# Retention and a four-expert layer on one core: where a batch's remainder is issued, and how a head pair's small matmuls are grouped

## The chip, the core and the metric

The kernel runs on one core of one Trainium2 chip. The metric is the device time in microseconds of one execution; less is better. Engines: TensorE (PE in the profile; its weight loads are PEld), VectorE (DVE), ScalarE (ACT), GpSimd (POOL) and SyncE (SP), which here only issues DMAs.

## The reference

Two stages, one feeding the other. Eight batches, eight heads, 576 positions, head size 64:

```python
scores = scale * np.matmul(q, k.transpose(0, 1, 3, 2))
gamma = 1.0 - 2.0 ** (-5.0 - np.arange(H))
Dmat = np.where(rel >= 0, gamma[:, None, None] ** rel[None, :, :], 0.0)
x = np.matmul(scores * Dmat[None], v)        # then heads side by side: [4608, 512]
p = domain_probs / (domain_probs.sum(-1, keepdims=True) + 1e-09)
for e in range(4):
    out += p[:, e:e + 1] * (np.maximum(x @ w1[e], 0.0) @ w2[e])
```

w1 is 512 x 1024 and w2 1024 x 512 for each of the four experts; rel is the distance of two positions.

## The kernel before

**Retention.** The decay gamma to the power of a distance is split into a factor for k (`gk`) and one for q (`gq`, applied to the output), so that within a chunk only a triangular mask is left. A batch's 576 positions are four chunks of 128 and a *remainder* of 64. Heads go in pairs, a head in each half of the 128 partitions. A `Pair` has these steps:

- `cast` (L227 on): k times gk to bf16 on VectorE, q and v to bf16 on ScalarE; `trans_dma`: SP issues two transposing DMAs into `qkT`.
- `scores` (L253): eight 64-row matmuls into a PSUM tile `s`, which VectorE masks into `sT` (L261).
- `kv` (L242): eight 64-column matmuls of running k^T v sums into a PSUM tile `kvp`, copied by ScalarE in two halves into the *states* `sbd` (L251).
- `values` (L265): into a PSUM tile `o`, eight matmuls of v with sT (L270) and then three of a state with q (L273), which add what earlier chunks contribute; VectorE multiplies by gq into `xt` (L280).

`Rem` does the same for the remainders of a batch's eight heads at once (scores L305, mask L306, values L311 and L313, `xt` L317). Batches 0 and 1 are done by `Unit`, four heads and two chunks at a time, with the same steps (L469 to L576).

**The experts.** Tokens go in nine tiles of 512. A tile takes 16 up groups, each eight 128x512 matmuls into one PSUM tile `ph` (L326; in tile 1 sixteen of 128x256, L344), evicted with Relu into `h` by ScalarE in tile 0 (L330) and by VectorE with the mixing weight `pB` in the others (L332, L347). Then the down products follow. Tile 0 has for each expert two groups of 16 matmuls, `po` (L359), between the up groups, evicted by VectorE into `acc` (L367, L369). The other tiles use a seven-product scheme on 256-token halves (`Down`): products 1, 4, 2, 5, 6, 3, 7, each 16 matmuls of 128x256 (L429), accumulate in one PSUM tile `pd` for a half; the sums of h that they need are made on VectorE (`sums`, L404 to L410). The corresponding sums of w2 are made once, on VectorE (`w_sum`, L378 to L384), while tile 0 ends and tile 1 begins.

**The order of the work.** Nothing is reordered by a planner (`tc.manual_schedule()`): each engine executes its instructions in the order in which the program issues them, and waits where a tile isn't ready. The program issues one group or product after another, and after the n-th it runs the functions put into *slot* n. A dictionary `slots` with hand-written numbers thus places every step of the retention between the groups of the experts. Tile 0 has 24 slots (per expert four up groups and two po groups), the other tiles 30 (16 up groups, then 14 products). While tile t is computed, the pairs of batch t + 1 and the remainder of batch t are done, since they give the columns of the tile after it.

In tile 0 the remainder of batch 0 is cast in slot 11, its scores in slot 15 and its values in slot 16; batch 1's units follow from slot 14 on, with SP's loads of the mixing weights `pB` for tile 1 in slot 17 (`load_p`).

**PSUM.** All these PSUM tiles come from one ring of four (`ring`, two banks each). A tile is handed on when its last reader has finished; `pd` holds one of the four for seven products.

**DMA.** SP's loads, transposes and stores go through one queue (q1), GpSimd's loads of weights and of x for batch 1 through another (q0).

Of the kernel before, what the change touches and what calls it, by code (L numbers as in the profile page):

```python
# [23 lines left out]
def kernel(  # L24
# [10 lines left out]
    nc = tc.nc  # L35
    B, H, S, D = q.shape
    N, E = moe_domain_probs.shape
# [3 lines left out]
    C = 128  # L41
    NC = 4
    SM = NC * C
    R = S - SM
    NP = H // 2
# [20 lines left out]
    def ring_tile(name, shape, dt=FP32):  # L66
        return ring.tile(shape, dt, tag="ring", name=name)
# [5 lines left out]
    def load_pair(t, b, p, eng=nc.sync):  # L73
        for n, src in srcs:
            for j in range(2):
                eng.dma_start(out=t[n][:, :, j, :],
                              in_=src[b, 2 * p + j, 0:SM, :].rearrange("(c p) d -> p c d", p=C))

    def load_rem(b, eng=nc.sync):
        for j in range(2):  # L80
            for n, src in (("k", k), ("v", v)):
                eng.dma_start(out=rawr[n][64 * j:64 * j + 64, :, j, :],  # L82
                                  in_=src[b, j:H:2, SM:S, :].rearrange("g t d -> t g d"))
        eng.dma_start(out=rawr["q"][0:R, :, :, :].rearrange("t g j d -> t (g j) d"),
                          in_=q[b, :, SM:S, :].rearrange("h t d -> t h d"))
# [5 lines left out]
    sbd = const.tile([128, NP, NC, 128], BF16, name="sbd")  # L91
# [117 lines left out]
    def load_p(t, e, eng):  # L209
        pB[t, e] = ppool.tile([128, NT], FP32, tag="pB", name="pB")  # L210
        eng.dma_start(out=pB[t, e], in_=pd[e:e + 1, t * NT:(t + 1) * NT].to_broadcast([128, NT]))  # L211
# [4 lines left out]
    def xt_of(t):  # L216
        if t not in xt:
            xt[t] = xpool.tile([128, NDC, NT], BF16, tag="xt", name="xt")
        return xt[t]


    class Pair:
# [39 lines left out]
                self.sT[:, :, :, :].rearrange("p j c t -> p (j c) t"), s[:, :, :, :].rearrange("p j c t -> p (j c) t"),  # L262
                tri[:, :].unsqueeze(1).to_broadcast([128, 2 * NC, C]), op=MULT)

        def values(self):  # L265
            b, p = self.b, self.p
            o = ring_tile("o", [128, SM])
            for c in range(NC):
                for j in range(2):
                    nc.tensor.matmul(o[64 * j:64 * j + 64, c * C:(c + 1) * C], lhsT=self.bf["v"][:, c, j, :],  # L270
                                     rhs=self.sT[:, j, c, :], start=(c == 0), stop=False, skip_group_check=True)
            for c in range(1, NC):
                nc.tensor.matmul(o[:, c * C:(c + 1) * C], lhsT=sbd[:, p, c - 1, :], rhs=self.qkT[:, 0, c, :],  # L273
                                 start=False, stop=(c == NC - 1), skip_group_check=True)
            n0 = b * S
            a = 0
            while a < SM:
                t = (n0 + a) // NT
                z = min(SM, (t + 1) * NT - n0)
                nc.vector.tensor_tensor(xt_of(t)[:, p, n0 + a - t * NT:n0 + z - t * NT], o[:, a:z],  # L280
                                        gq[:, p, a:z], op=MULT)
                a = z
# [37 lines left out]
    def up_group(h, t, e, i):  # L320
        ph = ring_tile("ph", [128, 2, NT])
        x = xt_of(t)
        for f in range(2):
            fc = 2 * i + f
            for dc in range(NDC):
                nc.tensor.matmul(ph[:, f, :], lhsT=w1_sb[e][:, dc, fc * 128:(fc + 1) * 128],  # L326
                                 rhs=x[:, dc, :], start=(dc == 0), stop=(dc == NDC - 1))
        fk = e * NFC + 2 * i
        if t == 0:
            nc.scalar.activation(h[:, fk:fk + 2, :], ph, Relu)  # L330
            return
        nc.vector.scalar_tensor_tensor(h[:, fk:fk + 2, :], ph, 0.0,  # L332
                                       pB[t, e][:, :].unsqueeze(1).to_broadcast([128, 2, NT]), op0=MAX, op1=MULT)
        if i == NFC // 2 - 1 and t + 1 < n_nt:
            load_p(t + 1, e, nc.gpsimd)

    def up_half(h, t, half, e, i):
        ph = ring_tile("ph", [128, 4, NT // 2])
        x = xt_of(t)
        c = slice(256 * half, 256 * half + 256)  # L340
        for f in range(4):
            fc = 4 * i + f
            for dc in range(NDC):
                nc.tensor.matmul(ph[:, f, :], lhsT=w1_sb[e][:, dc, fc * 128:(fc + 1) * 128],  # L344
                                 rhs=x[:, dc, c], start=(dc == 0), stop=(dc == NDC - 1))
        fk = e * NFC + 4 * i
        nc.vector.scalar_tensor_tensor(h[:, fk:fk + 4, c], ph, 0.0,  # L347
                                       pB[t, e][:, c].unsqueeze(1).to_broadcast([128, 4, NT // 2]), op0=MAX, op1=MULT)
        if half == 1 and i == 1:
            load_p(t + 1, e, nc.gpsimd)  # L350
# [280 lines left out]
    h = hp.tile([128, E * NFC, NT], BF16, name="h")  # L631


    def attention(slots, b, at):
        add = lambda i, f: slots.setdefault(i, []).append(f)
        for p, (c, s, o) in enumerate(at):
            x = Pair(b, p)
            add(c, lambda x=x: [x.cast(raw1, n) for n in "kqv"])
            add(c, x.trans_dma)
            if p + 1 < NP:  # L640
                add(c, lambda p=p: load_pair(raw1, b, p + 1))
            elif b + 1 < B:
                add(c, lambda: load_pair(raw1, b + 1, 0))
            add(s, x.scores)
            add(s, x.kv)
            add(o, x.values)

    def remainder(slots, b, at):
        add = lambda i, f: slots.setdefault(i, []).append(f)
        x = Rem(b)  # L650
        l, c, s, o = at
        if b > 0:
            add(l, lambda: load_rem(b))
        add(c, x.cast)
        add(c, x.trans_dma)
        add(s, x.scores)
        add(o, x.values)

    def run(slots, i):
        for f in slots.get(i, []):  # L660
            f()

    slots = {}
    add = lambda i, f: slots.setdefault(i, []).append(f)
    remainder(slots, 0, (-1, 11, 15, 16))

    def v_cast(u):
        vs[u].cast()
        vs[u].trans_dma()
        if u == 0:  # L670
            load_v(2, nc.gpsimd)
        elif u == 2:
            load_v(3, nc.gpsimd)
        elif u == 3:
            load_pair(raw1, 2, 0)

    def v_head(u):
        vs[u].scores()
        vs[u].kv()

    for u, (c, sc, o) in enumerate(((14, 18, 19), (17, 21, 22), (21, 24 + 0, 24 + 2), (24 + 0, 24 + 4, 24 + 6))):
        add(c, lambda u=u: v_cast(u))
        add(sc, lambda u=u: v_head(u))
        add(o, lambda u=u: vs[u].values())
    add(17, lambda: [load_p(1, e, nc.sync) for e in range(E)])
    for j in range(4):
        for wi, which in enumerate((3, 1, 2, 4)):
            add((17, 19, 22, 25)[j] + wi // 2, lambda which=which, j=j: w_sum(which, 4 * j, 4 * j + 4))
# [13 lines left out]
    for t in range(1, n_nt):  # L702
        slots = {i - 24: f for i, f in slots.items() if i >= 24} if t == 1 else {}
        if t < B:
            remainder(slots, t, (-1, 1, 6, 8) if t > 1 else (-1, 6, 10, 11))
        if t + 1 < B:
            attention(slots, t + 1, ((5, 10, 12), (10, 15, 17), (15, 19, 21), (19, 23, 25)) if t > 1 else
                      ((9, 14, 16), (14, 19, 21), (19, 23, 25), (23, 27, 28)))
        d = [Down(h, t, s) for s in range(2)]
        add = lambda i, f: slots.setdefault(i, []).append(f)  # L710
        add(12, lambda: d[0].sums(1, 0, HK))
        add(13, lambda: d[0].sums(2, 0, HK))
        add(14, lambda: d[0].sums(4, 0, HK))
        add(15, lambda: d[0].sums(1, HK, KH))
        add(16, lambda: d[0].sums(2, HK, KH))
        add(16, lambda: d[0].sums(4, HK, KH))
        add(17, lambda: d[0].sums(3, 0, HK))
        add(17, lambda: d[0].sums(3, HK, KH))
        for i, which in enumerate((1, 2, 4, 3)):
            add(19 + i, lambda which=which: d[1].sums(which, 0, HK))  # L720
            add(19 + i, lambda which=which: d[1].sums(which, HK, KH))
        run(slots, -1)
        n = 0
        for e in range(E):
            for i in range(4):
                if t == 1:
                    up_half(h, t, n // 8, n % 8 // 2, n % 2)
                else:
                    up_group(h, t, e, i)
                run(slots, n)  # L730
                n += 1
        for s in range(2):
            for m in (1, 4, 2, 5, 6, 3, 7):
                d[s].product(m)
                run(slots, n)
                n += 1
# [30 lines left out]
```

## Time and profile before

| | |
|---|---|
| median of 3 runs | 557.69 us (557.51 to 559.37) |
| the profiled execution | 559.56 us |
| its span, first to last instruction | 557.8 us |
| mean granted TensorE clock | 0.992 |
| TensorE busy | 535.8 us (96%) |
| VectorE busy | 375.6 us (67%) |
| ScalarE, GpSimd busy | 110.7 us, 55.0 us |
| DMA: moved, mean | 64.28 MB, 115 GB/s |
| tiles 2 to 6, each | 58.2 us |

"Busy" of TensorE counts from the start of a matmul to its modelled end, and matmuls overlap, so short distances between matmuls are read from their starts. In the profile a group of instructions is named by its line in the program, its engine, its operation, its output and inputs; "L259 PE MATMUL s<-qkT 64*128" is the matmul of line 259 with the array used as 64 rows by 128 columns. A wait is put down to what ended it.

### The profile page before, as it was taken

The numbers are of one execution on the slowest core, as the hardware profiler recorded it, in microseconds if no ns is written. First come the engines' busy times: TensorE is split into PE (matmuls) and PEld (weight loads), VectorE is DVE, ScalarE is ACT, GpSimd is POOL, SyncE is SP. The second block draws the span as 40 slices with busy tenths as digits, with TensorE's granted clock in tenths as the row PEclk, the third lists the DMA queues.
The fourth block names the chain that finished last, engine by engine and source line by source line (L and its number), as shares of the span: only waits on it lengthen the run. The fifth ranks groups of instructions, "written<-read, shape, count | busy, mean of one in ns | idle before, by whom it ended". The sixth has DMA issues, their size and how long they took to land.

```text
span 557.8 us, 10528 instructions
## 1 busy us (share of the span) xinstructions
PE 535.8 (96%) x4388; PEld 351.6 (63%) x4416; DVE 375.6 (67%) x550; ACT 110.7 (20%) x216; POOL 55.0 (10%) x95
## 2 busy tenths in 40 slices
PE   4999599999999999999999999999999999999996
PEld 3544245888854686468645874588447854884485
DVE  4622067988668874897389838984788567736871
ACT  5323323203211220212013201231113100000010
POOL 4613101010000000000000000000000000000000
PEclk9999899999999999999999999999999999999999
DMA  9999918456735752577155724753367131010010
GB/s 240 211 206 252 163 42 212 100 112 140 174 90 122 157 137 75 119 133 171 58 117 130 145 89 97 152 134 95 92 136 146 50 98 41 20 58 19 1 39 38
DMA packets 147454, 64.28 MB, mean 115 GB/s; under 512 B 127216, under 2 KB 137584, under 8 KB 147408
## 3 DMA queue, kind: packets, MB, share of 16 engines
q1 hardware_dynamic: 137760, 44.35, 35.2%
q0 software_dynamic: 9648, 19.27, 15.8%
q8 instruction: 34, 0.56, 0.4%
q14 instruction: 12, 0.10, 0.1%
HBM read 53.56 MB, written 9.51 MB: 113 GB/s over the span
## 4 chain that ended last, share of the span: by engine, by line
PE 91%; DMA 3%; DVE 2%; ACT 1%; issue 1%; SPq 1%; POOL 0%; POOLq 0%; DVEq 0%; ACTq 0%
PE ph L326 36%; PE pd L429 35%; PE po L359 5%; PE ph L344 5%; DMA qTr<-bfr_q 2%; PE kvp L246 2%; PE o L270 1%; PE s L259 1%; PE o L273 1%; PE kvp L525 1%; DMA rawr_q<-in_q_dram 1%; PE pt L483 1%; PE s L506 1%; ACT gq L157 1%; SPq L82 0%
## 5 line engine op out<-in xcount | busy, mean ns | idle before, releaser
L326 PE MATMUL ph<-xt,w 128*128 128x512 bf16 x1000 | 226.7, 381 | 1.4 <-DVE xt L570 0.2
L326 PEld LDWEIGHTS <-w 128*128 128x128 bf16 x1024 | 99.1, 98 | 115.1 <-issue 2.4
L332 DVE SCALAR_TENSOR_TENSOR h<-ph,pB 128x1024 bf16<-128x1024 f32 x112 | 136.2, 1221 | 31.6 <-PE ph L326 31.4
L429 PEld LDWEIGHTS <-h 128*128 128x128 bf16 x1024 | 98.8, 98 | 12.2
L429 PEld LDWEIGHTS <-s 128*128 128x128 bf16 x768 | 74.3, 98 | 8.9
L429 PE MATMUL pd<-wx,h 128*128 128x256 bf16 x512 | 61.2, 273 | 0.0
L429 PE MATMUL pd<-wx,s 128*128 128x256 bf16 x512 | 61.1, 273 | 0.0
L251 ACT ACTIVATE sbd<-kvp 64x256 bf16<-64x256 f32 x48 | 18.1, 378 | 112.1 <-PE kvp L246 111.8
L261 DVE TENSOR_TENSOR sT<-s,tri 128x1024 bf16<-128x1024 f32 x24 | 29.2, 1215 | 11.2 <-PE s L259 11.2
L211 POOL DMA_DIRECT2D pB<-pd x28 | 15.2, 542 | 206.3 <-DVE h L332 159.4
L455 POOL TENSOR_TENSOR ob<-v,p 128x256 f32<-128x256 f32 x16 | 11.6, 724 | 231.7 <-DVE v L452 139.4
L359 PE MATMUL po<-wx,h 128*128 128x512 bf16 x124 | 30.7, 401 | 0.2
L429 PE MATMUL pd<-t2w,s 128*128 128x256 bf16 x256 | 30.6, 273 | 0.0
L429 PE MATMUL pd<-t4w,h 128*128 128x256 bf16 x256 | 30.6, 273 | 0.0
L446 DVE TENSOR_TENSOR u<-pd,p 128x256 f32<-128x256 f32 x16 | 6.7, 422 | 35.4 <-issue 29.5
L429 PE MATMUL pd<-t3w,h 128*128 128x256 bf16 x256 | 30.6, 273 | 0.0
L344 PE MATMUL ph<-xt,w 128*128 128x256 bf16 x256 | 29.2, 273 | 0.3 <-DVE h L347 0.3
L280 DVE TENSOR_TENSOR xt<-o,gq 128x384 bf16<-128x384 f32 (+6 forms) x48 | 18.0, 415 | 16.4 <-PE o L273 16.4
L344 PEld LDWEIGHTS <-w 128*128 128x128 bf16 x256 | 24.6, 98 | 3.4 <-issue 0.3
L437 ACT ACTIVATE p<-pd 128x256 f32<-128x256 f32 x16 | 6.1, 384 | 96.1 <-PE pd L429 74.5
L330 ACT ACTIVATE h<-ph 128x1024 bf16<-128x1024 f32 x16 | 16.4, 1023 | 39.8 <-PE ph L326 38.0
L408 DVE TENSOR_TENSOR h<-h 128x1024 bf16<-128x1024 bf16 x32 | 23.4, 770 | 0.0
(130 smaller groups left out, 418.8 us busy)
## 6 DMA issues: line engine op xcount, KB each, us to landing
pB<-pd POOLq DMA_DIRECT2D x28, 256.0 KB, 3.7
raw_k<-in_k_dram SPq DMA_DIRECT2D x48, 128.0 KB, 2.9
raw_q<-in_q_dram SPq DMA_DIRECT2D x48, 128.0 KB, 3.4
raw_v<-in_v_dram SPq DMA_DIRECT2D x48, 128.0 KB, 3.3
w<-in_moe_w_dram POOLq DMA_DIRECT2D x4, 1024.0 KB, 13.5
wx<-in_moe_w_dram POOLq DMA_DIRECT2D x4, 1024.0 KB, 16.6
out_dram<-oa SPq DMA_DIRECT2D x16, 256.0 KB, 2.0
out_dram<-ob SPq DMA_DIRECT2D x16, 256.0 KB, 2.0
```

Source lines behind the costliest of these rows:

```text
L211: eng.dma_start(out=pB[t, e], in_=pd[e:e + 1, t * NT:(t + 1) * NT].to_broadcast([128, NT]))
L251: nc.scalar.activation(sbd[r, self.p, :, r], kvp[r, :, :], Copy)
L261: nc.vector.tensor_tensor(self.sT[:, :, :, :].rearrange("p j c t -> p (j c) t"), s[:, :, :, :].rearrange("p j c t -> p (j c) t"), tri[:, : ...
L280: nc.vector.tensor_tensor(xt_of(t)[:, p, n0 + a - t * NT:n0 + z - t * NT], o[:, a:z], gq[:, p, a:z], op=MULT)
L326: nc.tensor.matmul(ph[:, f, :], lhsT=w1_sb[e][:, dc, fc * 128:(fc + 1) * 128], rhs=x[:, dc, :], start=(dc == 0), stop=(dc == NDC - 1))
L330: nc.scalar.activation(h[:, fk:fk + 2, :], ph, Relu)
L332: nc.vector.scalar_tensor_tensor(h[:, fk:fk + 2, :], ph, 0.0, pB[t, e][:, :].unsqueeze(1).to_broadcast([128, 2, NT]), op0=MAX, op1=MULT)
L344: nc.tensor.matmul(ph[:, f, :], lhsT=w1_sb[e][:, dc, fc * 128:(fc + 1) * 128], rhs=x[:, dc, c], start=(dc == 0), stop=(dc == NDC - 1))
L359: nc.tensor.matmul(po[:, g, :], lhsT=h[:, e * NFC + fc, ns * 128:(ns + 1) * 128], rhs=wx[e // 2][:, (e % 2) * NFC + fc, :, :].rearrange("p ...
L408: nc.vector.tensor_tensor(h[:, l, self.b], h[:, l, self.a], h[:, l, self.b], op=SUB)
L429: mm = nc.tensor.matmul(dst, lhsT=src[:, kk, tok], rhs=rhs(c), start=(start and c == 0), stop=(c == KH - 1), skip_group_check=True)
L455: nc.gpsimd.tensor_tensor(self.ob[:, HF:Dm], self.v, self.p5, op=ADD)
```

## The change

Three edits.

1. The remainder of batch 0 is cast in slot 12 in place of 11, its scores are issued in slot 18 in place of 15, its values in slot 19 in place of 16. Unit 0 of batch 1 moves one slot back, from 18 and 19 to 19 and 20, so as to stay behind it. The four loads of pB for tile 1 move from slot 17 to slot 15.
2. `values` issues its three state matmuls first. It is given the next pair, and between the states and the eight matmuls with sT it issues that pair's scores and k^T v.
3. `attention` takes the slots of the casts and of these blocks apart: the first pair's scores and k^T v alone, then three joined blocks, then the last pair's values alone. In tiles 2 to 6 the casts stand in slots 5, 10, 15 and 20 (before: 5, 10, 15, 19) and the blocks in 10, 15, 20, 25 and 28 (before: scores in 10, 15, 19, 23, values in 12, 17, 21, 25). In tile 1 the casts stand in 8, 13, 18 and 22 and the blocks in 13, 18, 22, 26 and 28.

```diff
-        def values(self):
+        def values(self, following=None):
             b, p = self.b, self.p
             o = ring_tile("o", [128, SM])
+            for c in range(1, NC):
+                nc.tensor.matmul(o[:, c * C:(c + 1) * C], lhsT=sbd[:, p, c - 1, :], rhs=self.qkT[:, 0, c, :],
+                                 start=(c == 1), stop=False, skip_group_check=True)
+            if following is not None:
+                following.scores()
+                following.kv()
             for c in range(NC):
                 for j in range(2):
                     nc.tensor.matmul(o[64 * j:64 * j + 64, c * C:(c + 1) * C], lhsT=self.bf["v"][:, c, j, :],
-                                     rhs=self.sT[:, j, c, :], start=(c == 0), stop=False, skip_group_check=True)
-            for c in range(1, NC):
-                nc.tensor.matmul(o[:, c * C:(c + 1) * C], lhsT=sbd[:, p, c - 1, :], rhs=self.qkT[:, 0, c, :],
-                                 start=False, stop=(c == NC - 1), skip_group_check=True)
+                                     rhs=self.sT[:, j, c, :], start=False, stop=(c == NC - 1), skip_group_check=True)
...
-    def attention(slots, b, at):
+    def attention(slots, b, cast_at, head_at):
         add = lambda i, f: slots.setdefault(i, []).append(f)
-        for p, (c, s, o) in enumerate(at):
-            x = Pair(b, p)
+        xs = [Pair(b, p) for p in range(NP)]
+        add(head_at[0], xs[0].scores)
+        add(head_at[0], xs[0].kv)
+        for p in range(NP):
+            add(head_at[p + 1], lambda p=p: xs[p].values(xs[p + 1] if p + 1 < NP else None))
+        for p, c in enumerate(cast_at):
+            x = xs[p]
             add(c, lambda x=x: [x.cast(raw1, n) for n in "kqv"])
             add(c, x.trans_dma)
...
-            add(s, x.scores)
-            add(s, x.kv)
-            add(o, x.values)
...
-    remainder(slots, 0, (-1, 11, 15, 16))
+    remainder(slots, 0, (-1, 12, 18, 19))
...
-    for u, (c, sc, o) in enumerate(((14, 18, 19), (17, 21, 22), (21, 24 + 0, 24 + 2), (24 + 0, 24 + 4, 24 + 6))):
+    for u, (c, sc, o) in enumerate(((14, 19, 20), (17, 21, 22), (21, 24 + 0, 24 + 2), (24 + 0, 24 + 4, 24 + 6))):
...
-    add(17, lambda: [load_p(1, e, nc.sync) for e in range(E)])
+    add(15, lambda: [load_p(1, e, nc.sync) for e in range(E)])
...
-            attention(slots, t + 1, ((5, 10, 12), (10, 15, 17), (15, 19, 21), (19, 23, 25)) if t > 1 else
-                      ((9, 14, 16), (14, 19, 21), (19, 23, 25), (23, 27, 28)))
+            attention(slots, t + 1, *(((5, 10, 15, 20), (10, 15, 20, 25, 28)) if t > 1 else
+                                          ((8, 13, 18, 22), (13, 18, 22, 26, 28))))
```

## The prediction, made before the change was run

> **What bounds the kernel now.** I read the page's first part, then TensorE's waits, then the stretch of the longest wait, then one steady tile. The page says that TensorE is busy nearly throughout and that the chain of work is TensorE's.
>
> ```profile
> PE 535.8 (96%) x4388; PEld 351.6 (63%) x4416; DVE 375.6 (67%) x550; ACT 110.7 (20%) x216; POOL 55.0 (10%) x95
> ...
> PE 91%; DMA 3%; DVE 2%; ACT 1%; issue 1%; SPq 1%; POOL 0%; POOLq 0%; DVEq 0%; ACTq 0%
> ```
>
> So only three things can shorten it: TensorE waiting, its clock, and what it pays between matmuls. TensorE's list of waits has one large entry outside the start-up:
>
> ```profile
> PE sr L305 <- DMA qTr<-bfr_q: 7.5, 2, 6.8
> ...
> PE o L547 <- DVE sT L508: 0.3, 1, 0.3
> ```
>
> It is the remainder of batch 0 waiting for its transposed q. The stages around it (stretch, length, PE, PEld, DVE, ACT, POOL busy, granted clock, DMA share, GB/s):
>
> ```profile
> 59.40:66.40 7.00, 0.25 (x3) 0.08 (x3) 0.00 (x0) 2.51 (x5) 1.49 (x2) 0.85 1.30 155
> 66.40:72.20 5.80, 5.80 (x20) 2.28 (x21) 0.42 (x1) 0.00 (x0) 0.00 (x0) 0.60 0.27 74
> 72.20:76.00 3.80, 3.75 (x25) 1.88 (x25) 1.74 (x3) 0.00 (x0) 0.00 (x0) 1.00 0.02 4
> ```
>
> The reader is to see two losses: 6.75 us without matmuls, and after it a granted clock of 0.60, in which sixteen po matmuls take 5.70 us instead of 3.46 (427 ns from start to start, then 216). In the steady tile, TensorE's timeline around one pair (start, duration, count):
>
> ```profile
> 301.64 0.81 PE L326 MATMUL ph<-xt,w 128*128 128x512 bf16 x3
> 302.38 0.40 PE L259 MATMUL s<-qkT 64*128 64x128 bf16 x8
> 302.71 0.47 PE L246 MATMUL kvp<-bf_v,bf_k 128*64 128x256 bf16 x8
> ...
> 306.40 0.38 PE L429 MATMUL pd<-t4w,h 128*128 128x256 bf16 x2
> 306.71 0.41 PE L270 MATMUL o<-sT,bf_v 128*64 128x128 bf16 x8
> 307.06 0.34 PE L273 MATMUL o<-qkT,sbd 128*128 128x128 bf16 x3
> 307.23 0.27 PE L429 MATMUL pd<-wx,h 128*128 128x256 bf16 x1
> ```
>
> The third field after the line is the shape in which the array is used. The last ph starts at 302.07 and lasts 0.216, so s could start at 302.29; it starts at 302.38. The pd before the values could be followed at 306.62; o starts at 306.71. Within a shape two heads' matmuls follow at 53 ns; from s to kvp it is 146, from the values to the states 151. From the states back to pd, both 128*128, it is 56, the states' own time. A change of shape thus costs some 0.09 us, a return to the same shape nothing.
>
> [...] 0.09 us at each change, none where the shape stays. [...] 6.75 us idle, then 427 for 216 ns, for about 4.4 us. [...] the four transposes that SP issued from 54.76 to 59.47 land only from 64.6 to 68.2, beside GpSimd's weight and x loads.
>
> **The change, part by part.**
>
> *Remainder of batch 0 (cast 11 to 12, scores 15 to 18, values 16 to 19).* From the last ph of the third expert (59.44) to the next expert's first (75.92) there are 16.48 us. The work in it: 32 po at 0.216 = 6.91, the scores 0.18, the values 0.23, sum 7.32. Lost: 9.1 us, 6.75 of waiting, 2.24 of clock and 0.1 of restarting. After the change the scores stand behind two po groups and one ph group: 59.44 + 6.91 + 1.73 = 68.1. Do the transposes land by then? The k cast on VectorE has nothing else to wait for in slot 12 (TensorE's groups there are evicted by ScalarE), so it stays at 54.05. The q cast moves behind one Relu, from 46.74 to about 55.5, ends at 56.1, and SP reaches qTr at 56.16 anyway, since kTr occupies it until 56.06. So qTr lands at about 66.3, 1.8 us before its use. The next transposes (batch 1's first unit, landing 68.2) are used in slot 19, at 70.2. **Gain 9.1 us.** Cover: if these landings slip by over 1.8 us, the rest comes back as waiting.
>
> *What is late next.* The fourth expert now starts 9 us earlier against VectorE. From 66.6 it has the slot-17 acc (1.3), a k cast (0.6), two weight sums (1.3): 69.8, then sTr (0.4) at 70.2, while TensorE wants sTr at 70.0. I take **+0.3 us** (bounds 0 and 0.8, one more weight sum ahead). Unit 0's sT follows at about 73.0 and is wanted at 73.2; unit 1's transposes are issued at about 68 and 69.4 and wanted at 75.3.
>
> *The four pB loads (slot 17 to 15).* They need nothing that is late. SP issues them at 61 instead of 80.8, for 1.95 us, ahead of unit 1's transposes; SP is idle there. One MB took about 5 us in the trace (82 to 86). They follow the four transposes on SP's queue and share with two x loads until about 71, where DMA lay idle from 69 to 78. Unit 1's transposes then land near 74, 1.3 us early. I take **0**, bounds 0 and +1.
>
> *One block per pair.* Six batches with four pairs: before, 24 score blocks and 24 value blocks. Now the first scores and last values stand alone, and 18 blocks join the values of one pair with the scores of the next. States first continue the 128*128 shape; the values follow k^T v in the same 128*64 shape. Removed per joined block: one entry into the values (0.09) and one return from k^T v (125 ns where 53 is the pace, 0.07): 0.17 us, at most 0.19. **Gain 18 x 0.17 = 3.1 us** (2.9 to 3.4), all on TensorE, so on the path. A block takes 0.82 + 0.61 - 0.17 = 1.26 us. No matmul is added; VectorE's and ScalarE's evictions are the same, later by some slots.
>
> *The wait that it adds.* The ring has four PSUM tiles. In slot 15 of tiles 2 to 6 the block takes three (o, s, kvp), so the first product, in slot 16, needs that of the last ph group. Its eviction cannot end before 0.20 (a group that ended at 292.21 has its eviction start at 292.41) + 1.22 = 1.42 us after the group; with the sums ahead of it VectorE's timeline has
>
> ```profile
> 301.96 0.68 DVE L410 TENSOR_TENSOR s<-h,s 128x1024 bf16<-128x1024 bf16 x1
> 302.56 1.22 DVE L332 SCALAR_TENSOR_TENSOR h<-ph,pB 128x1024 bf16<-128x1024 f32 x1
> ```
>
> an end at 303.78, 1.49 after the group's 302.29. The block covers 1.26. With 0.06 for the signal TensorE waits **0.3 us in each of five tiles: +1.5**. Behind it stands everything, TensorE being in order. Bounds: 0, and 0.75 where the tile handed on is kvp's (two ScalarE copies of 0.38 after k^T v). Other blocks lie in the product stage, where the next product keeps its tile; tile 1's first block too.
>
> *Casts and buffers.* A pair's cast is now issued after the block that reads its buffers; the v cast and the transposes wait for that block, but ScalarE and VectorE are held to TensorE there by their evictions. Cast to scores stays five slots (four for tile 1's last two), over 8.7 us. The last values move from slot 25 to 28; slot 29 (1.75 us) and three ph matmuls cover their 0.76 us eviction. 0.
>
> *Sum.* -9.1 - 3.1 + 1.5 + 0.3 = -10.4. The profiled execution took 559.56 (span 557.8), giving 549.2; the median of the runs is 557.69, 1.87 below it, giving **547.3 us**. Bounds: 557.69 - 9.1 - 3.4 = 545.2; 557.69 - 9.1 - 2.9 + 3.8 + 0.8 + 1.0 = 551.3.
>
> **The rivals.**
>
> *The wait moves to unit 1.* The pB loads stand ahead of its transposes. If those then take the 10.0 us that qTr took, they land at 79.4, 4 us late, enough for the clock to drop again (another 2.2): 547.3 + 6.2 = 553.5. For it: such a landing did occur. Against: then a 1 MB weight load and several x loads were in flight, now only two x loads. 0.10.
>
> *The joined block saves nothing,* [...]: 547.3 + 3.1 = 550.4. Against: states to pd shows 56 ns. 0.10.
>
> *Slower: every block waits for VectorE.* Place: the first matmul after a block, or the block's own o, if the tile it needs is that of s or of an older o. VectorE ends sT 2.6 us and xt 3.3 us after the group, 1.3 to 2.0 beyond the block: 18 x 1.3 = 23.4, so 557.7 - 12.2 + 23.4 + 0.3 = 569.2. It decides from 12.2 / 18 = 0.68 us per block. Against: at 13 of 18 blocks the next matmul opens no tile, and before the change TensorE shows no wait for a steady tile's PSUM. 0.03.
>
> **How the numbers follow.** Forecast 0.77, rivals 0.10, 0.10, 0.03. The range 545.2 to 551.3 takes in the forecast's bounds and the second rival; about 0.15 is left out. Half a per cent (554.9 to 560.5) is what a measurement can tell from no change: faster 0.95, same 0.02, slower 0.03.
>
> **What would show it.** No TensorE wait at L305 near 68 us and a granted clock of 1.00 from 30 to 90 us; the fourth expert's first ph near 66.4; in a joined block kvp to o at about 53 ns and ph to o without a gap; a wait of 0.3 us before the first pd in tiles 2 to 6, on the eviction of ph. Wrong if unit 1's scores wait for qkT, or if the wait at pd is over 0.7 us.

## The result, and the profile after

The changed kernel takes a median of **551.84 us** (four runs: 550.04, 550.35, 553.33, 553.64) where the kernel before took 557.6 (four runs, 557.31 to 559.37): a ratio of 0.989, 95% interval 0.9843 to 0.9937. So it is faster by more than half a per cent, as forecast, but the median lies 0.5 us above the range (545.2 to 551.3) and 4.5 above the 547.3 predicted. The profiled execution is the one of 550.04 us, span 548.2, granted clock 1.0; it stands against 559.56 before. In the changed kernel the lines behind `values` are numbered 3 higher; within it the states' matmuls are L269 and those with sT L276.

The first part of the page, and its chain of work:

```profile
PE 530.7 (97%) x4388; PEld 354.1 (65%) x4416; DVE 376.4 (69%) x550; ACT 110.1 (20%) x216; POOL 55.4 (10%) x95
...
PE 74%; DMA 8%; DVE 7%; SPq 5%; ACT 3%; issue 2%; POOL 0%; POOLq 0%; another core or an unknown queue 0%; ACTq 0%; DVEq 0%
```

TensorE is still busy nearly throughout, but its share of the chain fell from 91% to 74%: the chain now leaves it at several small waits and goes back through VectorE, the loads and SP. TensorE's waits from the first expert on (in all, times, longest):

```profile
PE pd L432 <- DVE h L335: 1.7, 5, 0.8
PE sr L308 <- DMA qTr<-bfr_q: 0.5, 1, 0.5
...
PE pd L432 <- ACT p L440: 0.3, 1, 0.3
PE s L509 <- DMA qkT<-bf_q: 0.3, 1, 0.3
PE pd L432 <- ACT oa L443: 0.3, 1, 0.3
```

The 6.75 us are gone. What is left of `sr` (0.5, before 0.7) is the remainder of a later batch. In its place stand five waits of the first product of a tile for VectorE (four of 0.22 us and one of 0.83), and single ones of 0.3 us. The three stretches shown of before, now:

```profile
59.40:66.40 7.00, 6.96 (x33) 3.00 (x32) 1.41 (x2) 2.53 (x5) 1.49 (x2) 1.00 1.21 222
66.40:72.20 5.80, 5.28 (x62) 2.91 (x62) 5.36 (x10) 2.05 (x2) 0.00 (x0) 1.00 1.17 182
72.20:76.00 3.80, 3.75 (x33) 1.68 (x34) 3.68 (x6) 1.78 (x3) 0.00 (x0) 1.00 0.59 168
```

In the first, TensorE is busy 6.96 of 7.00 us where it was 0.25; in the second the clock is 1.00 where it was 0.60. The DMA engines, nearly idle in the third row before, are now loaded until past 72 (third row: share 0.59, before 0.02). A joined block in tile 3, from TensorE's timeline:

```profile
233.58 0.81 PE L329 MATMUL ph<-xt,w 128*128 128x512 bf16 x3
234.23 0.33 PE L269 MATMUL o<-qkT,sbd 128*128 128x128 bf16 x3
234.49 0.40 PE L259 MATMUL s<-qkT 64*128 64x128 bf16 x8
234.82 0.47 PE L246 MATMUL kvp<-bf_v,bf_k 128*64 128x256 bf16 x8
235.12 0.39 PE L276 MATMUL o<-sT,bf_v 128*64 128x128 bf16 x8
235.73 0.27 PE L432 MATMUL pd<-wx,h 128*128 128x256 bf16 x1 [0.22 <-DVE h L335]
```

The last ph starts at 234.01 (the group's first, 233.58, and two more at 0.216) and would end at 234.23, where the states begin: no gap on entry. From the first k^T v matmul to the first of the values it is 0.30 us; before, to the product that followed, it was 0.40 (302.71 to 303.11). From the start of the last k^T v matmul to the values it is 25 ns now, and was 125. The bracket at the end is the wait that the change adds.

From the first ph of one tile to the next (us):

| | tiles 0 and 1 | tiles 2 to 5, each | tile 6 | tile 7 | the rest |
|---|---|---|---|---|---|
| before | 133.28 | 58.23 | 59.14 | 52.43 | 50.34 to the start of the last product |
| after | 124.66 | 57.83 (one 58.88) | 58.97 | 52.21 | 50.34 |

That is -8.62, -0.55, -0.17 and -0.22: -9.56 of the span's 9.6. Tile 0 alone went from 69.97 to 61.57. (Tile 6 took 59.14 before, not the 58.2 that the table ahead of the change gives for tiles 2 to 6.)

### The profile page after: what moved, and what is told of

It is laid out like the page before. It is cut to its first block, busy times and chain, and to the rows that moved or that the text cites. A ratio compares the mean times of both kernels' runs of the same rounds, so it can differ in the third digit from the quotient of the medians.

```text
span 548.2 us, 10530 instructions
## 1 busy us (share of the span) xinstructions
PE 530.7 (97%) x4388; PEld 354.1 (65%) x4416; DVE 376.4 (69%) x550; ACT 110.1 (20%) x216; POOL 55.4 (10%) x95
## 4 chain that ended last, share of the span: by engine, by line
PE 74%; DMA 8%; DVE 7%; SPq 5%; ACT 3%; issue 2%; POOL 0%; POOLq 0%; another core or an unknown queue 0%; ACTq 0%; DVEq 0%
PE pd L432 32%; PE ph L329 29%; PE po L362 4%; DVE h L335 4%; PE ph L347 3%; DMA raw_v<-in_v_dram 3%; SPq L76 2%; DMA qkT<-bf_q 2%; SPq L239 2%; PE kvp L528 1%; DMA raw_k<-in_k_dram 1%; PE kvp L246 1%; PE o L276 1%; PE s L259 1%; PE s L509 1%
## 5 line engine op out<-in xcount | busy, mean ns | idle before, releaser
L432 PE MATMUL pd<-wx,s 128*128 128x256 bf16 x512 | 61.2, 273 | 0.1
L261 DVE TENSOR_TENSOR sT<-s,tri 128x1024 bf16<-128x1024 f32 x24 | 29.3, 1220 | 16.6 <-PE s L259 16.6
L362 PE MATMUL po<-wx,h 128*128 128x512 bf16 x125 | 28.5, 379 | 0.2
L372 DVE SCALAR_TENSOR_TENSOR acc<-po,pm,acc 128x512 f32<-128x512 f32 x12 | 8.5, 746 | 24.0 <-PE po L362 24.0
```

Source lines behind the costliest of these rows:

```text
L261: nc.vector.tensor_tensor(self.sT[:, :, :, :].rearrange("p j c t -> p (j c) t"), s[:, :, :, :].rearrange("p j c t -> p (j c) t"), tri[:, : ...
L362: nc.tensor.matmul(po[:, g, :], lhsT=h[:, e * NFC + fc, ns * 128:(ns + 1) * 128], rhs=wx[e // 2][:, (e % 2) * NFC + fc, :, :].rearrange("p ...
L432: mm = nc.tensor.matmul(dst, lhsT=src[:, kk, tok], rhs=rhs(c), start=(start and c == 0), stop=(c == KH - 1), skip_group_check=True)
```

## The theory, and what could be wrong with it

My theory after this result: the mechanism is the one forecast, and the pair of profiles (-9.5 against -10.4) bears it out; the median is higher because in part of the executions a wait returns in tile 0, at batch 1's unit 0 or with its clock. Rivals: that the pB loads, moved ahead, cause it (the first rival of the prediction, at another place); that the joined blocks or the PSUM ring cost more than one profile shows; that the first four runs were an accident. The experiments ran on several chips; each is compared with the kernel before on its own chip. They go by labels: a1 to a4, b1 to b4, c1 to c4, d1 and d2, in the order in which they stand here. A "wait at L509" is that of TensorE at unit 0's scores.

## Experiments: each part alone

**The changed kernel again** (a1, no edit).

> The changed kernel once more, unaltered. Its four runs stood at 550.0 and 550.4 us with a granted clock of 1.00 and at 553.6 and 553.3 us with 0.992 and 0.993. Theory C (a half-clock stretch that falls into some executions): the runs come again in two groups about 3.3 us apart, and the group goes with the clock. Theory D (late loads or stores of SP, no clock): the times spread without a gap and the clock doesn't order them.

Measured: 549.68 us (six runs, 549.28 to 554.3) against 559.29, ratio 0.9859 (0.982 to 0.9898). In four of the six the mean granted clock is 0.998 to 1.0 and the time 549.3 to 549.7; the other two are 551.93 (clock 0.997) and 554.3 (0.992). So the spread is real, and in these six the clock orders the times. The two groups 3.3 us apart don't come again as such, and over more runs the clock alone doesn't order them: c1 below has 553.68 us at 0.997 and 552.23 at 0.995, so waits count beside it.

**The remainder alone** (a2): the kernel before with the three edits of tile 0.

```diff
-    remainder(slots, 0, (-1, 11, 15, 16))
+    remainder(slots, 0, (-1, 12, 18, 19))
-    for u, (c, sc, o) in enumerate(((14, 18, 19), (17, 21, 22), ...
+    for u, (c, sc, o) in enumerate(((14, 19, 20), (17, 21, 22), ...
-    add(17, lambda: [load_p(1, e, nc.sync) for e in range(E)])
+    add(15, lambda: [load_p(1, e, nc.sync) for e in range(E)])
```

> Kernel before with the remainder of batch 0, unit 0 and the pB loads moved, pairs untouched. My steps: the 6.75 us wait and the 2.24 us of half clock go, up to 0.3 comes back behind sTr: tile 0 (to the first ph of tile 1) from 69.97 to about 61.2 us, the whole some 8.5 us shorter, 548.5 to 549.5. If the half-clock stretch comes from the joined blocks, this kernel has one group of times only; if it comes from the start of the kernel or from the first tile, it has two.

Measured: 552.25 us (551.28 to 557.21), ratio 0.9896 (0.9859 to 0.9932): -7.0 us. Its tile 0 takes 61.56 us, as in the changed kernel (61.57); the tiles after it take what they took before. The forecast of 548.5 to 549.5 was missed: the 8.5 us were again taken from a median. Between the two profiled executions (559.56 and 551.28) they are 8.3. One of the six runs stands at 557.21 with a clock of 0.993, so slow executions come without joined blocks, too.

**The joined blocks alone** (a3): the changed kernel with those three lines put back.

> Kernel before with the joined blocks alone, remainder at its old slots. My steps: 18 x 0.17 us less, about 0.3 us of waiting in each of tiles 2 to 6: tiles of 57.8 in place of 58.2 us, the whole 1 to 2 us shorter (555.5 to 556.5). If a shape change costs nothing that a joined block can save: 1.5 us longer than before. If late SP loads bite (the 0.8 us wait of tile 4 in the changed kernel), one or more tiles are 58.9.

Measured: 557.12 us (555.05 to 560.59), ratio 0.9971 (0.9954 to 0.9989): -2.2 us. The two parts add up: -7.0 - 2.2 = -9.2, together -9.6 (a1), within what the intervals allow. Tiles 3, 5 and 6 take 57.83 us each, as forecast (57.8). The wait at the remainder, which this version keeps, can be read in its profiled execution, which took 555.05; first from TensorE's waits, then from two stretches:

```profile
PE sr L308 <- DMA qTr<-bfr_q: 4.8, 2, 4.4
```

```profile
59.50:65.00 5.50, 1.07 (x10) 0.38 (x8) 0.27 (x1) 2.81 (x5) 1.49 (x2) 1.00 1.19 193
65.00:68.50 3.50, 3.50 (x10) 1.27 (x9) 0.15 (x1) 0.00 (x0) 0.00 (x0) 0.51 0.44 108
```

The same wait is 4.4 us here, not 6.75, and is followed by 3.5 us at a clock of 0.51, where the trace of before has 6.83 us at 0.50 (from 64.25); tile 0 takes 67.39 us, not 69.97. Tile 0 is the same code in both. The size of the loss that the change removes differs from one execution to the next.

**The pB loads back in slot 17** (a4), in the changed kernel.

```diff
-    add(15, lambda: [load_p(1, e, nc.sync) for e in range(E)])
+    add(17, lambda: [load_p(1, e, nc.sync) for e in range(E)])
```

> Changed kernel with the four pB loads back in slot 17. My step: they cost nothing at 15, so within 0.3 us of the changed kernel. Rival (the loads stand ahead of unit 1's transposes): unit 0's scores wait 0.3 us less for qkT, and up to 1 us is gained; or the loads now stand behind unit 1's transposes and nothing moves.

Measured: 551.29 us (548.1 to 554.41), ratio 0.9861 (0.9822 to 0.99), where the changed kernel had 0.9859 on the same chip (the median is 1.6 us higher, the mean of the six runs 0.3). The spread stays. Unit 0's transposes land 11.3 to 13.0 us after their issue with the loads late, 12.0 to 13.8 with them early (a1). Moving the pB loads is worth nothing that can be measured, and they are not what delays unit 0.

## Experiments: the small waits

**The first half's x loads issued four slots later** (b1), in all tiles with attention. In the changed kernel the last pair's cast stands in slot 20, where the first stores also fall due. SP's timeline in tile 4 of the changed kernel:

```profile
306.15 1.19 SPq L239 DMA_TRANSPOSE qkT<-bf_k  x1
307.44 1.21 SPq L239 DMA_TRANSPOSE qkT<-bf_q  x1
308.71 1.12 SPq L76 DMA_DIRECT2D raw_k<-in_k_dram  x2
309.88 1.91 SPq L76 DMA_DIRECT2D raw_q<-in_q_dram  x2
311.88 1.00 SPq L76 DMA_DIRECT2D raw_v<-in_v_dram  x2
312.99 0.45 SPq L452 DMA_DIRECT2D out_dram<-oa  x1
```

and what waits for that store on ScalarE:

```profile
315.84 0.38 ACT L443 ACTIVATE oa<-pd 128x256 f32<-128x256 f32 x1 [5.83 <-DMA out_dram<-oa]
```

The store of oa is issued after two transposes and six loads, 6.8 us after the first of them; ScalarE waits 5.83 us for oa's buffer, and its next eviction of pd (0.3 us on TensorE here, up to 1.1 in a4) comes late.

```diff
-                add(c, lambda: load_pair(raw1, b + 1, 0))
+                add(c + 4, lambda: load_pair(raw1, b + 1, 0))
```

> Changed kernel with the six loads of the next batch's first pair issued four slots later, behind the stores of the first half of a tile. Theory S (the stores stand on SP's queue behind the last pair's transposes and these loads, which the change moved one slot closer to them; ScalarE's copy oa waits for the store, and the product after it for the copy): the waits of TensorE on oa and p, 0.3 to 1.6 us in the four traces with joined blocks, go. If the store itself is slow to land, they stay.

Measured: 552.8 us, one run. SP now issues the store right behind the transposes:

```profile
310.60 1.21 SPq L239 DMA_TRANSPOSE qkT<-bf_q  x1
311.90 0.53 SPq L452 DMA_DIRECT2D out_dram<-oa  x1
313.60 2.00 SPq L76 DMA_DIRECT2D raw_k<-in_k_dram  x2
```

and in tiles 2 to 6 the waits on oa and p are gone; one of 0.3 us on p is left. The time says nothing on that: this execution had a wait of 2.6 us at L509 with half clock after it (eight ph matmuls take 3.3 us from 74.24 on, the eight from 78.03 on 1.8). All nine traces with joined blocks and without this edit have a wait on oa or p; of the four with it (b1, b4, c4, d2) only b1 has one, the 0.3 us.

**The second block one slot later** (b2), so that it doesn't stand just before the first product.

```diff
-            attention(slots, t + 1, *(((5, 10, 15, 20), (10, 15, 20, 25, 28)) if t > 1 else
+            attention(slots, t + 1, *(((5, 10, 16, 20), (10, 16, 20, 25, 28)) if t > 1 else
```

> Changed kernel with the first joined block of tiles 2 to 6, and the cast of the third pair, in slot 16 in place of 15, so that the first product has its PSUM tile before the block takes three. My step (the block's three tiles leave the product only that of the last ph): the five waits of 0.22 us for VectorE's h, 1.1 us in all and 1.7 us where a load came late, go, tiles of 57.6 in place of 57.8 us. If they belong to VectorE's backlog and not to the ring, they reappear at the next product.

Measured: 548.61 us, one run. The five waits of the first product for h are gone; TensorE's list from 140 us on is

```profile
PE sr L308 <- DMA qTr<-bfr_q: 0.7, 1, 0.7
PE pd L432 <- ACT oa L443: 0.4, 1, 0.4
PE s L259 <- DMA qkT<-bf_q: 0.3, 1, 0.3
```

and a steady tile takes 57.56 us, not 57.83. The wait is thus worth 0.27 us per tile, and the three joined blocks alone (58.23 - 57.56) / 3 = 0.22 us each.

**Remainder and units one slot later still** (b3) in tile 0.

```diff
-    remainder(slots, 0, (-1, 12, 18, 19))
+    remainder(slots, 0, (-1, 12, 19, 20))
-    for u, (c, sc, o) in enumerate(((14, 19, 20), (17, 21, 22), ...
+    for u, (c, sc, o) in enumerate(((14, 20, 21), (17, 22, 23), ...
```

> Changed kernel with the scores and values of the remainder and of units 0 and 1 one more slot back. Theory L (the slow executions are those in which the transposes of tile 0 land late, so that TensorE waits and the clock drops): wait for qkT of 0.3 to 0.8 us gone, no run above 552 us, median near 549. Theory C (a half-clock stretch with no wait of its own behind it): one run in three still near 553.5 us with a clock of 0.992.

Measured: 550.21 us (four runs, 549.18 to 550.47), ratio 0.9822 (0.9775 to 0.987). The runs lie close together, but the profile contradicts the expectation: in the execution of 550.44 us the wait at L509 is not gone but 2.0 us, since unit 0's transposes landed 14.6 us after issue, 1 to 3 us later than in the changed kernel's first two traces; and unit 1's values, now in the last slot of tile 0, make the next tile's first group wait 1.1 us for xt. More distance alone didn't cure it.

**All four edits at once** (b4: the three above, and the pB loads in slot 17).

> All of it: the later loads, the block in slot 16, the remainder one more slot back, and the pB loads in slot 17. Sum of the waits that they should take out of the changed kernel's profile: 0.6 (oa, p) + 1.7 (h) + 0.3 (qkT) + 0.2 (sTr), 2 to 3 us: 547 us, where the clock stays at 1.00. If the waits only move, 549 to 550.

Measured: 548.97 us (547.58 to 552.26), ratio 0.9811 (0.9773 to 0.9849). TensorE's waits from 60 to 90 us:

```profile
PE s L509 <- DMA qkT<-bf_q: 2.7, 1, 2.7
PE ph L347 <- DVE xt L573: 1.1, 1, 1.1
```

The steady tiles are clean; tile 0 isn't.

## Experiments: why unit 0's transposes land late

**The changed kernel a third time** (c1), on another chip.

> The changed kernel a third time, to stand beside the next kernel on the same chip. Theory L (unit 0's transposed q lands late in some executions; TensorE waits, and where the wait is long the clock drops): some runs near 549.5 us, some 2 to 5 us above. A trace of a slow one shows the wait at unit 0's scores.

Measured: 554.17 us (550.38 to 555.12), ratio 0.9889 (0.9853 to 0.9925). Its profiled execution, of 552.23 us, shows the event. TensorE's timeline, then two stretches:

```profile
68.56 1.89 PE L329 MATMUL ph<-xt,w 128*128 128x512 bf16 x8
...
72.24 0.42 PE L509 MATMUL s<-qkT 64*64 64x128 bf16 x16 [1.56 <-DMA qkT<-bf_q]
```

```profile
66.00:73.80 7.80, 5.92 (x65) 3.11 (x64) 6.35 (x10) 2.53 (x4) 0.00 (x0) 1.00 1.17 207
73.80:77.30 3.50, 3.50 (x26) 1.36 (x25) 1.60 (x4) 1.30 (x2) 0.00 (x0) 0.51 0.38 80
```

A wait of 1.56 us, then 3.5 us at a clock of 0.51, which lose half of that, 1.7 us. Against the execution a1 showed (a wait of 0.79 there and no drop) that makes 0.77 + 1.7 = 2.5; its tile 0 took 64.19 us against 61.49, and the whole 552.23 against 549.72. No execution of the changed kernel above 552.23 us was traced; that the seven runs from 553.3 to 555.1 lose their time in the same way, with a longer wait or a second stretch, is not shown.

**Unit 2's x loads left out**, in the changed kernel (c2) and in the kernel before (c3). Unit 2 then works on unit 0's data.

```diff
-        if u == 0:
-            load_v(2, nc.gpsimd)
-        elif u == 2:
+        if u == 2:
             load_v(3, nc.gpsimd)
```

> Changed kernel that leaves out the three x loads for unit 2 (768 KB, issued by GpSimd from 55 to 61 us; unit 2 then works on unit 0's data), which share the DMA engines with the remainder's and unit 0's transposes. Theory L: those transposes land earlier, unit 0's scores never wait over 0.3 us, and the runs stay within 1.5 us of their fastest, near 549. If the slow executions have another cause (the start of the kernel, stores, the clock by itself): the same spread as the changed kernel, up to 554.

> Kernel before without the same three loads. Theory L: its long wait is the landing of the remainder's transposes, so it shrinks from 6.8 us (to 3 or 4, since the weight load of expert 3 is still in flight), and with it the clock's stretch: 554 to 556.5 us, with less spread than the 556.5 to 562.7 of the kernel before. If the loads don't matter: the same 559.

Measured: the changed kernel without them 548.48 us (five runs, 547.69 to 549.45), ratio 0.9802 (0.977 to 0.9834); the kernel before without them 557.04 (556.09 to 560.08), ratio 0.9956 (0.994 to 0.9972). In the first there is no wait at unit 0's scores, its transposes land 5.5 to 7.0 us after their issue, and tile 0 takes 61.03 us. Its slowest run is faster than the fastest of c1, on the same chip, where unit 0's transposes took 12.7 to 13.0 us. In the second the wait at the remainder is still

```profile
PE sr L305 <- DMA qTr<-bfr_q: 5.1, 2, 4.5
```

So these loads delay unit 0's transposes in the changed kernel. Leaving them out is worth 2.6 us to the kernel before. Its wait was 6.75 us in one trace with these loads and 4.4 in another (a3), so the 4.5 here doesn't show that they lengthen it; but it stands without them, too: for that the remainder had to be moved.

**The same loads on SP's queue** (d1), behind unit 0's transposes, in the changed kernel. Nothing is left out; the bytes are the same.

```diff
         if u == 0:
-            load_v(2, nc.gpsimd)
+            load_v(2, nc.sync)
```

> Changed kernel with unit 2's three loads issued by SP, behind unit 0's transposes, in place of GpSimd. If the loads delay the transposes [...]: unit 0's transposed q lands 6 to 8 us after its issue as without the loads (12 to 17 us in the changed kernel), no wait at unit 0's scores, all runs between 547.5 and 550 us. If it is the bytes: still late landings in some executions, runs up to 554 us.

Measured: 549.79 us (six runs, 549.1 to 550.79), ratio 0.9832 (0.9804 to 0.9861). The spread shrank from 5.0 us (a1) and 4.7 (c1) to 1.7, and all six have a clock of 0.998 to 1.0. Three of the six lie a little above the 547.5 to 550 that was expected. The changed kernel wasn't run on this chip, and the intervals of the ratios overlap; what differs is the spread. There is no wait at L509. Unit 0's transposes, which took 12.7 to 13.0 us from issue to landing in c1, take here

```profile
DMA to landing us min/median/max: 4.8/5.6/6.4
```

The stretches from 66 to 74 us show the same; in c1

```profile
66.00:70.00 4.00, 3.68 (x21) 1.61 (x20) 3.52 (x6) 1.02 (x1) 0.00 (x0) 1.00 1.17 106
70.00:74.00 4.00, 2.44 (x47) 1.64 (x45) 3.02 (x6) 1.71 (x3) 0.00 (x0) 0.98 1.18 310
```

and with the loads on SP's queue

```profile
66.00:70.00 4.00, 4.00 (x24) 1.88 (x22) 2.80 (x5) 1.02 (x1) 0.00 (x0) 1.00 0.96 315
70.00:74.00 4.00, 3.81 (x53) 1.95 (x51) 3.96 (x7) 1.78 (x3) 0.00 (x0) 1.00 0.34 70
```

In c1 the DMA engines are as full from 66 to 70 us (share 1.17) but move 106 GB/s: unit 0's transposes, issued at 57.1 and 59.2, are still running and land at about 70 and 72. Their packets are small: in the trace of before, from 62 to 66 us, SP's queue, on which only transposes were issued from 54.76 to 78.19, moved 0.28 MB in 1150 packets, some 240 bytes each. In d1 they are through by 66.3, and the loads of x and pB run at 315 GB/s four microseconds earlier. In c1 both queues moved packets from 50 to 80 us, GpSimd's for 53.7% of the engines' time and SP's for 46.1%; how an engine divides its time between them was not shown. What the two traces show is the landing: at the median 5.6 us after issue with the loads behind the transposes on one queue, 12.8 with them on the other. They don't separate the order from the kind of queue, as GpSimd's was replaced by SP's, nor from the time: the first of the loads is issued at 61.2 us here and at 55.3 in c1.

**The best put together**: the x loads four slots later, the second block one later, the remainder in slots 19 and 20 with units (14, 20, 21) and (17, 21, 22), pB in slot 17; then the same with unit 2's loads on SP's queue (c4 and d2).

> All of b4 but unit 1 at its slots of the changed kernel, so that the tile-1 wait of 1.1 us for its xt, which b4's trace showed, goes: 1 us below b4 in the same circumstances, 547 to 548 us; by theory L still some runs 3 us above.

> The kernel of c4 with the same edit. Without the late landings its runs should all stand where its best three stood, 546.5 to 548 us; if the loads now come late for unit 2, a wait of 1 to 2 us appears at the start of tile 1 and it is 548 to 550.

Measured: the first 548.69 us (546.48 to 551.09), ratio 0.9806 (0.977 to 0.9842), with a wait in its profiled execution (550.77 us) of

```profile
75.18 0.42 PE L509 MATMUL s<-qkT 64*64 64x128 bf16 x16 [3.85 <-DMA qkT<-bf_q]
```

and the second **547.78 us** (546.79 to 548.14), ratio 0.9793 (0.9763 to 0.9824), the lowest median of all versions, with a spread of 1.35 us where the first has 4.6. The ratios don't tell the two apart. In its profile (546.79 us, span 545.1) TensorE waits from the first expert on for no more than

```profile
PE s L259 <- DMA qkT<-bf_q: 0.3, 1, 0.3
PE ph L347 <- DVE h L350: 0.3, 1, 0.3
PE sr L308 <- DVE bf_k L230: 0.2, 1, 0.2
```

## Why the prediction was right and wrong

547.3 us were predicted and 551.84 measured. Of the 4.5 us between them, 1.9 come from the last step of the sum (from 549.2 down to 547.3), 0.9 from its terms (549.2 against the 550.04 of the profiled execution) and 1.8 from the distance of the median from that execution, where the cover failed (the parts are rounded). Each in turn below.

**Remainder of batch 0: right.** -9.1 and +0.3 were forecast for tile 0; it went from 69.97 to 61.57, -8.4. No wait at the remainder, clock 1.00, the fourth expert's first ph at 66.57 where 66.4 was forecast. The +0.3 for sTr came as 0.2, and unit 0's scores waited 0.3 beside it.

**Joined block: right in kind, too small.** 0.17 us each was forecast, 0.22 measured (57.56 against 58.23 for three). The entry has no gap, as forecast; the return from k^T v to a matmul of the same shape gained 0.10 us where I took 0.07 (25 ns remain, not 53). So 18 blocks would gain 4.0, not 3.1; that holds for the 15 in tiles 2 to 6, while tile 1 with its three got only 0.22 shorter, not 0.67, which stays open. The rival that they save nothing falls: from the last k^T v matmul (128*64) the traces show 125 ns to the start of one of another shape (128*128) and 25 to one of the same.

**PSUM ring: right.** Five waits of the first product on the eviction of ph, 0.22 us in four tiles and worth 0.27 a tile by b2 (forecast 0.3); in one tile 0.83, where VectorE had waited 0.81 us for a raw_k that was loaded late. That one is over the 0.7 named as a sign of being wrong; b2 shows that the ring is its place, too. In tile 3 the eviction ends at 235.68 and TensorE starts at 235.73: 0.05 us for the signal, where 0.06 was taken. The rival that every block waits falls.

**"Casts and buffers ... 0": wrong.** A cast brings its DMAs. One slot later, the last pair's put two transposes and six loads on SP ahead of the first stores; ScalarE then waits for oa's buffer and TensorE for ScalarE, 0.6 us in this profile, up to 1.8 in others (a4). b1 removed all but 0.3. I had cost the cast on VectorE and ScalarE and not on SP.

**pB loads: right, 0** (a4). The first rival put the new wait at unit 1 behind these loads. Nothing waited there. Of its kind, though, an event came: a wait at unit 0's scores, and half clock behind it (1.56 us, then 3.5 us at 0.51 in c1).

**The cover: wrong, and with it the median moved by 1.8.** The prediction took from one trace that unit 0's transposes land at 68.2, 2.0 us before their use, and that the cover of the remainder is 1.8. That landing is not a constant. Issue to landing was 8.7 to 9.2 us in the trace of before, 11.5 to 13.2 in the first of the changed kernel, 15.4 in b4, up to 16.6 in c4: waits at L509 from none (a4) to 3.9 us, with or without 1.7 of clock behind them. Of the 16 runs of the changed kernel seven are between 549.3 and 550.4 and nine between 551.9 and 555.1. c2 against c1 shows that unit 2's x loads, issued from 55 to 61 us on the other queue, are a cause: without them none of five runs was above 549.5, where c1 had 550.4 to 555.1. In the twelve runs of d1 and d2 the same bytes did no such harm behind the transposes on SP's queue. The loads alone don't decide: with them, a2 and a3 had landings of 6.6 to 7.7. The text did name the condition ("if these landings slip by over 1.8 us, the rest comes back as waiting"), but gave it no chance and no place in the range.

**The last step of the sum: wrong.** From the profiled execution, -10.4 gave 549.2; measured in the pair, 550.04. I then took off another 1.87 because the median of the three runs lay that much below. But the loss that was removed is what those executions differ by. Of 76 runs of the kernel before over four sessions, those with a mean clock of 0.997 (11) average 557.2 us, those at 0.992 (24) 559.3 and those at 0.989 (16) 561.4. A stretch like that of a3, 3.5 us at a clock of 0.51, takes 0.003 off the mean clock of such a run (3.5 x 0.49 / 558), so these are, by estimate from that and from the mean clocks, runs with one, two and three times this loss (the last two also with some at the very end: a clock of 0.64 from 555.0 to 557.8 in the trace of before, another 0.002). The profiled execution had 0.992 and twice the loss, 6.83 us at 0.50; two of the three runs shown were some 2 us shorter, and so had less to win. The wait was 6.75 in one execution and 4.4 in another (a3). A loss that varies can't be taken whole from a median that holds only part of it: 549.2 was the estimate for an undisturbed execution, and 549.3 to 550.4 is what the seven fastest took. Without this step the same bounds would have reached 553.2.

**Open.** Why the same transposes land after 7 us in one execution and 13 in another (a2 and a3, with GpSimd's queue, had 6.6 to 7.7). Whether d1's cure is the order on one queue, that GpSimd's queue isn't used, or that the loads are issued later. c2 is 1.3 us below d1, on another chip; in the traces 0.6 of it lies in tile 0 and 0.75 in tile 1, and what in them causes it is not shown. No run was made on what exactly brings the clock down.

## What to carry to other kernels

Before you take a wait away on the strength of a landing in one trace, ask what else is in flight on the other queue at that time, and put the landing's spread, not its value, against the cover; here the transposes landed 5.6 us after issue with the loads behind them on one queue (d1), 12.8 with the loads on the other (c1). A loss that differs between executions (of the kernel before, the runs at a clock of 0.997 average 557.2 us, those at 0.989 561.4) is to be subtracted from the execution in which it was measured, not from the median. A step that is moved takes its DMAs with it: look at what they now stand ahead of on the issuing queue, stores included.

## What the runs showed of the hardware that was not expected

- Half clock stood for 6.83 us in the trace of before (64.25 to 71.08, clock 0.50), and for some 3.5 us in a3 (65.0 to 68.5), c1 (73.8 to 77.3) and c4 (75.8 to 79.3), each at a mean of 0.51. In c3 it shows in the matmuls: sixteen po in 5.1 us from 64.31 on, then sixteen in 3.45. The length of a wait alone doesn't settle whether it comes: it came within the wait of 6.75 us (before) and after those of 4.5 (c3), 4.4 (a3), 3.85 (c4), 2.63 (b1) and 1.56 (c1), but not after those of 2.0 (b3) and 2.72 (b4). What does settle it was not shown.
- Unit 0's transposes took 4.8 to 6.6 us from issue to landing with the 0.75 MB of x loads behind them on the same queue (d1, d2), and 6.6 (a3) to 16.6 (c4) beside them on the other queue.
- SP took about 1.2 us to issue a transpose and 0.5 to 1.0 for a load in tile 4 of the changed kernel; six loads and two transposes held a store back by 6.8 us.
